# Reordering SyncE's transfers and two attention stretches in a fused retention and bilinear FFN kernel

## The chip, the cores and the metric

One core of a Trainium2 chip. The metric is the time of the whole kernel on the device in microseconds (us). The profile times one execution in detail; its span is about 1.7 us shorter than the time measured around the kernel. The granted clock of TensorE is listed for each execution.

## The reference, cut to what matters

```python
# q, k, v: (8, 8, 576, 64) float32;  w_a, w_b: (512, 1536);  w_out: (1536, 512)
scores = scale * q @ k.T
ret = (scores * Dmat) @ v              # Dmat: gamma_h ** (i - j) for i >= j, else 0
x = ret.transpose(0, 2, 1, 3).reshape(4608, 512)
out = (x @ w_a) * (x @ w_b) @ w_out
```

## The kernel before

The FFN's products run in blocks of tokens (512, 256, 256, then 512 each). The attention of a *pair* (256 tokens of all heads) is placed among them by a list `todo`: each entry has a position, counted in full FFN products of 512 columns, and is emitted at the first edge at or after it. The prediction names products by their output: for each `F`, one of the 12 groups of 128 hidden columns, `pa` and `pb` are x times the two first weights; `po` is an output tile, 12 products over `F`. An edge lies behind each `pb` and behind every fourth product of a `po`. One pair goes through these steps:

- `load_pair`: q, k, v from HBM, issued on SyncE;
- `ahead`: GpSimd casts q, then k, to bf16, and scales v (the three in this order);
- `turn`: two DMA transposes (of q, then of k), also issued on SyncE;
- `stretch(into, outof)`: TensorE's small products, for two pairs at once.

```python
    def turn(n):
        ...
        for w in (0, 1):
            nc.sync.dma_start_transpose(
                qkT[:, w].rearrange("p k c s -> p (k c) s"), qkb[:, w])

    def stretch(into, outof):
        flush()
        ...
            from_states(outof, o, begun)                  # o <- qkT, states
            ...
            convert, convert_swapped = keyed(into, ...)   # kv <- vb, qkb
            masked = matched(into)                        # sc <- qkT, qkT
            ...
            scaled = from_keys(outof, o, begun)           # o <- sT, vb
            later.append(lambda: scaled(0))               # VectorE: xT <- o, a few products later
            later.append(lambda: scaled(1))
```

So the stretch of pairs 6 and 5 needs pair 6's scaled v for `keyed` and its transposes for `matched`, and it makes the x of pair 5, which block 3 (the first of 512 tokens after the two of 256) reads at its start.

## Time and profile before

| kernel before | |
|---|---|
| time, median of 3 (lowest to highest) | 333.75 us (333.65 to 334.54) |
| span of the profiled execution | 331.8 us |
| TensorE busy | 96% |
| its waits for data in the middle of the run | 1.32 us (pair 4's transposes), 1.38 us (block 3's x) |
| granted clock, mean of the profiled execution | 1.0 |
| time in 30 later executions, beside the experiments | 332.34 to 336.36 us |

A line of the timeline has the start, the length, the engine, what it does, and in brackets how long the engine sat idle before it and what ended that. SPq is SyncE issuing transfers. The lines on which the argument stands are in the prediction.

### The profile page before, as it was taken

What the parts mean: (1) busy time and instruction counts of PE and PEld (TensorE: products, weight loads), DVE (VectorE), ACT (ScalarE), POOL (GpSimd) and SP (SyncE); (2) the same over time, 40 slices, a digit from 0 to 9 for tenths busy, and PEclk for the clock granted to TensorE, in tenths of its full rate; (3) what the DMA queues carried; (4) which work ended last, traced back from release to release, by engine and by line L of the source; (5) the groups of instructions that cost most, each with busy time, mean ns of one, the idle gap of its engine ahead of it and who ended that gap; (6) DMA issues with size and microseconds to landing.
All of it is one profiled execution on the core that took longest, in us unless ns stands there. A gap on an engine that the chain in (4) does not pass through costs nothing.

```text
span 331.8 us, 8671 instructions
## 1 busy us (share of the span) xinstructions
PE 319.8 (96%) x3612; PEld 168.1 (51%) x3648; DVE 163.7 (49%) x292; ACT 128.6 (39%) x275; POOL 114.6 (35%) x146
## 2 busy tenths in 40 slices
PE   8999999989989999999999999999999999999996
PEld 4644456848634554545454545454445444444443
DVE  5734435664674465656265625662456246414321
ACT  7734744553543344343235313532332333213321
POOL 4870078835277274634063405360430000000000
DMA  8999999999999998992599258945850420031013
GB/s 220 248 172 208 236 227 222 225 166 234 199 205 254 214 215 200 206 219 54 140 224 213 61 127 188 224 71 149 180 116 4 138 54 0 2 95 34 1 26 100
DMA packets 143175, 50.37 MB, mean 152 GB/s; under 512 B 124576, under 2 KB 138656, under 8 KB 143136
## 3 DMA queue, kind: packets, MB, share of 16 engines
q1 hardware_dynamic: 138384, 45.10, 65.0%
q0 software_dynamic: 4752, 4.72, 8.7%
q8 instruction: 28, 0.46, 0.6%
q14 instruction: 11, 0.09, 0.1%
HBM read 37.75 MB, written 9.44 MB: 142 GB/s over the span
## 4 chain that ended last, share of the span: by engine, by line
PE 86%; DMA 5%; SPq 2%; issue 2%; DVE 2%; ACT 1%; POOL 1%; DVEq 0%; POOLq 0%; ACTq 0%
PE po L716 27%; PE pb L697 27%; PE pa L682 26%; SPq L153 2%; DMA vf<-in_v_dram 2%; DMA qf<-in_q_dram 2%; PE o L589 2%; PE o L602 1%; DMA qkT<-qkb 1%; PE sc L563 1%; PE kv L506 1%; PE kv L359 1%; DVE sums L526 0%; POOL qkb L440 0%; PE pa L664 0%
## 5 line engine op out<-in xcount | busy, mean ns | idle before, releaser
L702 DVE TENSOR_TENSOR hT<-ha,pb 128x512 bf16<-128x512 bf16 (+1 forms) x120 | 75.8, 633 | 99.6 <-PE pb L697 95.2
L690 ACT CAST ha<-pa 128x512 bf16<-128x512 f32 (+1 forms) x120 | 64.8, 543 | 122.7 <-PE pa L682 121.5
L697 PE MATMUL pb<-xT,wb_sb 128*128 128x512 bf16 (+1 forms) x474 | 111.5, 357 | 0.4
L682 PE MATMUL pa<-xT,wa_sb 128*128 128x512 bf16 (+1 forms) x459 | 108.4, 357 | 2.8 <-DVE xT L612 1.4
L716 PE MATMUL po<-wo_sb,hT 128*128 128x512 bf16 (+1 forms) x430 | 95.0, 373 | 1.8 <-issue 1.6
L697 PEld LDWEIGHTS <-wb_sb 128*128 128x128 bf16 x480 | 46.8, 98 | 46.4 <-issue 0.3
L682 PEld LDWEIGHTS <-wa_sb 128*128 128x128 bf16 x474 | 45.5, 98 | 46.7 <-issue 1.9
L716 PEld LDWEIGHTS <-hT 128*128 128x128 bf16 x444 | 42.3, 98 | 46.8
L440 POOL CAST qkb<-qf 64x1024 bf16<-64x1024 f32 x15 | 15.4, 1029 | 85.8 <-DMA qf<-in_q_dram 85.0
L445 POOL TENSOR_TENSOR vb<-vf,vs 128x1024 bf16<-128x1024 f32 x15 | 28.5, 1901 | 12.4 <-DMA vf<-in_v_dram 6.3
L727 DVE COPY osb<-po 128x512 f32<-128x512 f32 (+1 forms) x18 | 12.2, 676 | 40.7 <-PE po L716 40.7
L725 ACT COPY osb<-po 128x512 f32<-128x512 f32 (+1 forms) x19 | 10.9, 574 | 44.4 <-PE po L716 41.5
L526 DVE TENSOR_TENSOR sums<-kv,sums 128x256 f32<-128x256 f32 x46 | 19.5, 423 | 2.8 <-PE kv L506 0.8
L612 DVE TENSOR_TENSOR xT<-o,qs 128x512 bf16<-128x512 f32 x30 | 19.6, 682 | 2.5 <-PE o L602 2.5
L572 DVE TENSOR_TENSOR sT<-sc,mask 128x512 bf16<-128x512 f32 x30 | 19.4, 680 | 0.0
L444 POOL CAST qkb<-kf 64x512 bf16<-64x512 f32 x30 | 17.6, 614 | 0.9
L444 POOL CAST qkb<-qf 64x512 bf16<-64x512 f32 x30 | 17.6, 614 | 0.7
L440 POOL CAST qkb<-kf 64x1024 bf16<-64x1024 f32 x15 | 15.5, 1033 | 4.2 <-DMA kf<-in_k_dram 3.2
L530 ACT CAST states<-sums 64x512 bf16<-64x512 f32 x26 | 16.0, 617 | 0.3
L299 POOL CAST qkb<-kf 128x512 bf16<-128x512 f32 x5 | 3.1, 613 | 20.0 <-DMA kf<-in_k_dram 20.0
L740 PE MATMUL w<-ones 128*128 128x256 bf16 (+1 forms) x36 | 8.3, 359 | 1.5 <-DVE ones L197 1.5
L563 PE MATMUL sc<-qkT 64*64 64x64 bf16 x480 | 7.4, 195 | 1.3 <-DMA qkT<-qkb 1.3
(81 smaller groups left out, 155.7 us busy)
## 6 DMA issues: line engine op xcount, KB each, us to landing
qf<-in_q_dram SPq DMA_DIRECT2D x32, 256.0 KB, 4.5
kf<-in_k_dram SPq DMA_DIRECT2D x32, 256.0 KB, 5.1
vf<-in_v_dram SPq DMA_DIRECT2D x32, 256.0 KB, 5.1
out_dram<-osb SPq DMA_DIRECT2D x25, 256.0 KB, 2.2
out_dram<-osb SPq DMA_DIRECT2D x22, 128.0 KB, 2.4
wo_sb<-in_moe_w_out_dram POOLq DMA_DIRECT2D x3, 512.0 KB, 18.0
qf<-in_q_dram SPq DMA_DIRECT2D x8, 128.0 KB, 3.2
kf<-in_k_dram SPq DMA_DIRECT2D x8, 128.0 KB, 3.5
```

The costliest lines, as they stand in the source:

```text
L440: nc.gpsimd.tensor_copy(qkb[0:64, w], t[0:64])
L444: nc.gpsimd.tensor_copy(to[:, :, 1 - r], fro[:, :, r])
L445: nc.gpsimd.tensor_tensor(vb.rearrange("p (k h d) -> p k h d", k=2, h=H), vf.rearrange("p (k h d) -> p k h d", k=2, h=H), vs2[:, 2 if n in ...
L526: nc.vector.tensor_tensor(sums[:, i], own, prev, op=ALU.add)
L530: nc.scalar.copy(to(half(1 - r)), fro(half(r)))
L572: nc.vector.tensor_tensor(sT[:, on].rearrange("p c k s -> p (c k) s"), sc[:, on].rearrange("p c k s -> p (c k) s"), mask3.unsqueeze(1).to_ ...
L612: nc.vector.tensor_tensor(x_of(t0, 128).rearrange("p c (a s) -> p c a s", a=2), o[:, :, :, kp].rearrange("p a c s -> p c a s"), qs[:, :, s ...
L682: nc.tensor.matmul(pa[:, 0:n], wa_sb[:, c, fs], xT[:, c], start=(c == 0), stop=(c == NC - 1))
L690: nc.scalar.copy(ha[:, 0:n], pa[:, 0:n])
L697: nc.tensor.matmul(pb[:, 0:n], wb_sb[:, c, fs], xT[:, c], start=(c == 0), stop=(c == NC - 1))
L702: nc.vector.tensor_tensor(hT[:, F, 0:n], has[F][:, 0:n], pb[:, 0:n], op=ALU.mult)
L716: nc.tensor.matmul(po[:, 0:width], hT[:, F, u * 128:(u + 1) * 128], wo_sb[:, F, cols], start=(F == 0), stop=(F == NF - 1))
```

## The change

The intent: SyncE's order by need. Pair 4's transposes are to come first, then pair 5's v, block 0's stores, pair 5's transposes, pair 6's loads; and since data then come sooner, two stretches are placed 14 products sooner. (In the built program block 0's first two stores still stand ahead of pair 4's transposes.)

```diff
@@ output tile of a block
-                if (u + part) % 2 == 0:
+                if n == 256 or (u + part) % 2 == 0:
                     nc.scalar.copy(osb[:, cols], po[:, 0:width])
@@ first loads
-    for n in range(FIRST, FIRST + 3):
+    for n in (FIRST, FIRST + 1):
         load_pair(n)
+    load_pair(FIRST + 2, (Q, K))
@@ todo
-             (246, stretch, (5, 4)), (280, stretch, (6, 5)),
+             (232, stretch, (5, 4)), (266, stretch, (6, 5)),
-    casts = {3: 104, 4: 104.1, 5: 143, 6: 200, 7: 250, 8: 330}
-    turns = {4: 104.2, 5: 151, 6: 210, 7: 338, 8: 345}
+    casts = {3: 104, 4: 104.1, 5: 141, 6: 200, 7: 250, 8: 330}
+    turns = {4: 104.2, 5: 145, 6: 210, 7: 338, 8: 345}
-    todo += [(150, load_pair, (6, (0, 1))), (152, load_pair, (6, (2,)))]
+    todo += [(104.3, load_pair, (5, (V,))), (145.1, load_pair, (6, (K,))),
+             (145.2, load_pair, (6, (Q,))), (145.3, load_pair, (6, (V,)))]
```

The rest of the diff (cut) only keeps a pair's tiles in a dictionary, so that q, k and v may be loaded in any order.

More of the change, by code (lines that the diff above doesn't have):

```diff
@@ L136, in load_pair @@
             return
-        paired.setdefault(n, [])
+        paired.setdefault(n, {})
         for i in which:
@@ L145, in load_pair @@
                     src[b, :, s0:s0 + m, :].rearrange("h s d -> s h d"))
-            paired[n].append(t)
+            paired[n][i] = t
     def load_step(n, hh, which):
@@ L433, in ahead @@
     def ahead(n):
-        qf, kf, vf = paired.pop(n)
+        qf, kf, vf = (paired[n].pop(i) for i in (Q, K, V))
         qkb = nat.tile([128, 2, 2 * DM], BF16, tag="qkb", name="qkb2")
```

## The prediction

> **What bounds the kernel now.** I read the busy table first, then the list of what TensorE waited for, then the timelines of TensorE, SyncE and GpSimd between 60 and 95 us, where the diff acts.
>
> ```profile
> PE 319.8 (96%) x3612; PEld 168.1 (51%) x3648; DVE 163.7 (49%) x292; ACT 128.6 (39%) x275; POOL 114.6 (35%) x146
> ```
>
> TensorE is the bound, and nothing in the diff changes how many products it makes. So the change can only win what TensorE waits, and the list of its waits over the whole span is short:
>
> ```profile
> PE w L740 <- DVE ones L197: 1.5, 1, 1.5
> PE pa L682 <- DVE xT L612: 1.4, 1, 1.4
> PE sc L563 <- DMA qkT<-qkb: 1.3, 1, 1.3
> ```
>
> The first is the start of the program, which the diff leaves alone. The other two are the prize. The TensorE timeline shows where they are (columns: start, length, then in brackets the idle time before and what ended it):
>
> ```profile
> 68.38 0.44 PE L506 MATMUL kv<-vb,qkb 64*64 64x64 bf16 x32
> 70.14 0.45 PE L563 MATMUL sc<-qkT 64*64 64x64 bf16 x32 [1.32 <-DMA qkT<-qkb]
> ...
> 90.34 0.45 PE L589 MATMUL o<-qkT,states 64*64 64x64 bf16 x32
> 90.96 0.45 PE L563 MATMUL sc<-qkT 64*64 64x64 bf16 x32
> 94.88 1.02 PE L682 MATMUL pa<-xT,wa_sb 128*128 128x512 bf16 x4 [1.38 <-DVE xT L612]
> ```
>
> At 70.14 the stretch of pairs 4 and 3 waits for pair 4's transposes. At 94.88 the first 512-token block waits for the x that the stretch of pairs 6 and 5, begun only at 90.34, hands to VectorE. The SyncE timeline shows the order in which transfers were issued:
>
> ```profile
> 61.07 1.87 SPq L142 DMA_DIRECT2D vf<-in_v_dram  x2
> 63.04 1.46 SPq L653 DMA_DIRECT2D out_dram<-osb  x2
> 64.60 3.28 SPq L471 DMA_TRANSPOSE qkT<-qkb  x2
> 67.97 3.88 SPq L653 DMA_DIRECT2D out_dram<-osb  x6
> 71.91 2.03 SPq L142 DMA_DIRECT2D qf<-in_q_dram  x2
> 73.98 1.75 SPq L142 DMA_DIRECT2D kf<-in_k_dram  x2
> 75.84 3.67 SPq L471 DMA_TRANSPOSE qkT<-qkb  x2
> 79.57 1.26 SPq L142 DMA_DIRECT2D vf<-in_v_dram  x2
> 80.93 1.51 SPq L653 DMA_DIRECT2D out_dram<-osb  x2
> 82.61 3.40 SPq L471 DMA_TRANSPOSE qkT<-qkb  x2
> ```
>
> These are v of pair 5, stores, pair 4's transposes, stores, q and k of pair 6, pair 5's transposes, v of pair 6, stores, pair 6's transposes. GpSimd turns pair 6 into bf16 as it lands:
>
> ```profile
> 77.38 1.03 POOL L440 CAST qkb<-qf 64x1024 bf16<-64x1024 f32 x1 [8.35 <-DMA qf<-in_q_dram]
> 79.75 1.03 POOL L440 CAST qkb<-kf 64x1024 bf16<-64x1024 f32 x1
> 84.17 1.90 POOL L445 TENSOR_TENSOR vb<-vf,vs 128x1024 bf16<-128x1024 f32 x1 [2.16 <-DMA vf<-in_v_dram]
> ```
>
> So pair 6 is cast by 82.0 and its values are ready at 86.1; its transposes, issued at 82.61 and 84.52, land at 88.6. Its stretch needs them at 90.96: the slack there is only 2.4 us, and the diff spends it from both sides.
>
> **What the Trainium skill says.** "DMA: Bandwidth & Descriptors", section "Anatomy of one DMA": the DMA engines do not wait on semaphores; the wait stands on the issuing sequencer before dispatch. So a transpose that waits for GpSimd holds everything behind it on SyncE, as the gaps before the transposes here suggest. The same page, "Queues, rings and completion order": each engine consumes a ring in order[...]. The trace agrees: from 57 to 91 us SyncE's transfers land in the order of issue, and a 256 KB load about every 1.0 to 1.2 us. "Advanced Engine Details and Errata", section "X-Bar Transpose (TRN2)": transposes are as fast as regular transfers. The trace agrees roughly: from issue to landing 3.2 to 4.9 us, median 4.1, against 3.8 to 6.1 for loads of q. "TensorE: Matmul & The Clock Gate", "What's actually happening": the clock halves after an idle window of some 3.4 us. The waits here are shorter, the granted clock is 1.00, and sixteen 512-column products take 3.45 us, 0.216 us each.
>
> **The change part by part.** The counts of instructions stay. What moves:
>
> (a) v of pair 5 goes from ahead of pair 4's transposes to behind them. The two loads took the queue from 64.08 (k of pair 5 landed) to 66.19, so 2.1 us. Pair 4's transposes should land at 70.10 - 2.1 = 68.0. The scores could start at about 68.38 + 0.35 = 68.73 (the 0.35 is the distance from kv to scores in the stretch at 90.6). So the wait of 1.32 us goes, with 0.7 us to spare: **-1.3 us**. v of pair 5 lands near 70.5 and is scaled by 72.5; it is needed at about 76.7. No cost.
>
> (b) Pair 5's transposes go ahead of q and k of pair 6: issued at about 71.9 and 73.5, landing at about 75.5 and 76.9.
>
> (c) The stretch of pairs 5 and 4 goes from 246 to 232 products. It can only be placed at an edge, every 4 full products after a pb: it moves from behind the eighth to behind the fourth F of its block. The block began at 74.25, after (a) at 72.93; four F of 0.873 us put the stretch at 76.4 and its scores at about 77.0. The transposes of (b) land at 76.9 give or take 0.6. It just fits; I count **+0.2 us**.
>
> (d) The stretch of pairs 6 and 5 goes from 280 to 266, which is from F=3 of the second output tile to F=3 of the first, 12 products or 2.6 us. Without new waits it would start at 90.34 - 1.32 - 2.59 = 86.4. VectorE then has 20 products (4.3 us) before block 3. In the trace it takes 94.88 - 91.66 = 3.2 us from the stretch's end to x, and the copy of the output tile amid it moves to ScalarE. So the wait of 1.38 us goes: **-1.4 us**.
>
> (e) Pair 6's loads come behind pair 5's transposes, k ahead of q. The work in the queue up to q's end is the same as that up to pair 5's transposes before (81.43), so q lands at about 81.2 instead of 77.27, 3.9 us later. GpSimd casts q first and cannot start with k. Its casts keep their lengths: q 81.3 to 83.6, k to 86.0 (each 1.03 + 1.17 us and small gaps), values to 87.9. The second transpose, of k, is issued at 86.1, no sooner, and lands some 3.4 us later (the lag of the second transposes at 78.27 and 104.62 is 3.2 to 3.4): 89.5. The stretch wants its values at 86.7 and its scores at 86.4 + 0.6 = 87.0. It waits first for the values, 1.3 us, then for the transposes, **+2.5 us in all**. A wait that (c) adds is absorbed here, so it isn't counted twice.
>
> (f) The output copies of the 256-token blocks all go to ScalarE: two of 0.59 us instead of 0.69 us on VectorE. ScalarE is 39% busy; off the path.
>
> Sum: -1.3 - 1.4 + 2.5 = -0.2 us. Behind 95 us TensorE waited for almost nothing, so shifts there reach the end one to one. Pair 7's loads come 1.5 us later; its stretch is at 372 products, beyond 110 us, so that is hidden. The ledger says 333.75 - 0.2 = 333.55.
>
> **The rivals.** First: the order is right and pair 6 makes it; both waits go and none comes, 333.75 - 2.7 = 331.05. For it: the author had "need" in mind, and SyncE's issue was held up by a full queue in parts of 61 to 72 us (the same kind of load takes 0.57 to 2.2 us to issue), so all may run a microsecond sooner. Against: the chain q landed, cast q, cast k, transpose is 4.7 + 3.4 us long and would have to begin at 78.9. Second: the new wait is longer than what is won. If pair 5's transposes land late at 78 and push pair 6's loads too, or pair 6's transposes wait until GpSimd has done the values (87.9) and land at 91.5, the wait is over 4 us, and the time 335.3. A wait of that length could also brush the clock window. Third: pair 4's transposes are not sooner since the stores ahead of them set the pace; then (a) wins nothing and the gain in (d) is eaten all the same: 334.9.
>
> **Range and chances.** I put half on the ledger, 0.3 on the first rival or a half of it, 0.2 on the others, and lean a little to the better side: 333.2. The range is 330.8 to 335.2. Two per cent is 6.7 us; all waits that can be won make 2.7, so faster by over 2% is excluded in practice, and slower would need a wait of 9 us in pair 6's stretch. 0.01, 0.97, 0.02.
>
> **What would show it.** In the profile after: no wait of scores for qkT near 69 us and none of pa for xT at block 3 (a, d); pair 4's transposes landing near 68.0; GpSimd's first cast of pair 6 at about 81.3 and its values done at 87.9 (e); and a new wait in the stretch at about 86.5, of kv for vb and then of scores for qkT, together 2.5 us. If that wait is under 1 us, step (e) is wrong, by q's landing or by the transposes' lag. If the two old waits are still there, (a) or (d) is. If time moves behind 95 us, I missed a dependence of pair 7.

## The result

| | before | changed |
|---|---|---|
| time, median of 4 | 333.70 us | 338.02 us (336.27 to 338.87) |
| ratio | | 1.0121, 95% interval 1.0074 to 1.0168 |
| span of the profiled execution | 331.8 us | 335.9 us |
| mean granted clock of the four executions | 1.0 where profiled | 0.988, 0.990, 0.995, 0.990 |

Ratios, here and below, are the mean time of one kernel's runs over that of the other's of the same rounds, so not quite the ratio of the medians. The changed kernel is 1.2% slower: within 2%, but outside my range. A period of half clock, 3.41 us of some 335, takes 0.005 off the mean: so the execution with 0.995, the quickest (336.27 us), had one such period, the other three (337.6 to 338.87 us) two.

The list of TensorE's waits in the changed kernel (us in total, times, longest) has lost both old entries and got two new ones, 3.5 us together:

```profile
PE kv L506 <- POOL vb L445: 2.2, 1, 2.2
PE sc L563 <- DMA qkT<-qkb: 1.3, 1, 1.3
```

TensorE's timeline after the change: pair 4's scores at 68.58 and block 3 at 98.18 no longer wait; the stretch of pairs 6 and 5 begins at 86.46 and stands still twice.

```profile
68.58 0.56 PE L563 MATMUL sc<-qkT 64*64 64x64 bf16 x32
...
86.46 0.44 PE L589 MATMUL o<-qkT,states 64*64 64x64 bf16 x32
89.14 0.64 PE L506 MATMUL kv<-vb,qkb 64*64 64x64 bf16 x32 [2.23 <-POOL vb L445]
91.05 0.64 PE L563 MATMUL sc<-qkT 64*64 64x64 bf16 x32 [1.27 <-DMA qkT<-qkb]
...
98.18 1.03 PE L682 MATMUL pa<-xT,wa_sb 128*128 128x512 bf16 x4
```

SyncE's timeline after the change has the new order. Between 82.89 and 84.81 SyncE issues nothing: it waits for GpSimd before pair 6's first transpose.

```profile
61.77 2.76 SPq L471 DMA_TRANSPOSE qkT<-qkb  x2
64.59 2.31 SPq L142 DMA_DIRECT2D vf<-in_v_dram  x2
...
70.93 3.31 SPq L471 DMA_TRANSPOSE qkT<-qkb  x2
74.30 1.25 SPq L142 DMA_DIRECT2D kf<-in_k_dram  x2
75.60 1.90 SPq L142 DMA_DIRECT2D qf<-in_q_dram  x2
77.54 3.51 SPq L142 DMA_DIRECT2D vf<-in_v_dram  x2
81.15 1.74 SPq L653 DMA_DIRECT2D out_dram<-osb  x2
84.81 4.77 SPq L471 DMA_TRANSPOSE qkT<-qkb  x2
```

GpSimd's timeline after the change: it casts pair 6 from 82.54 on, where before it began at 77.38; its last line ends at 89.09, which is what kv waited for.

```profile
82.54 1.03 POOL L440 CAST qkb<-qf 64x1024 bf16<-64x1024 f32 x1 [10.06 <-PE pa L682]
84.84 1.03 POOL L440 CAST qkb<-kf 64x1024 bf16<-64x1024 f32 x1
87.19 1.90 POOL L445 TENSOR_TENSOR vb<-vf,vs 128x1024 bf16<-128x1024 f32 x1
```

(The releaser named in the first line, a product of TensorE, computes nothing that this cast reads; q of pair 6 landed at 82.39.) The chain that ended last runs over the same cast and the second transpose (start, length): issued at 87.14, landed at 91.01.

```profile
85.94 1.18 POOL qkb L444 x2
87.14 3.87 DMA qkT<-qkb
```

And there is a line on the page of the changed kernel that the page before does not have, the granted clock in 40 slices of 8.4 us:

```profile
PEclk9999999999779999999999999999999999999999
```

The clock's records put the drop at 88.91 us, to exactly 0.50, for 6.83 us, until 95.74. Asked for the three periods around it, the window view gives TensorE's busy time and, behind the engines, the granted clock:

```profile
85.50:88.91 3.41, 1.35 (x36) 0.64 (x36) 0.74 (x2) 0.38 (x2) 3.27 (x4) 1.00 0.70 109
88.91:92.32 3.41, 1.71 (x96) 1.57 (x97) 1.77 (x5) 0.00 (x0) 0.18 (x1) 0.50 0.88 139
92.32:95.74 3.42, 3.28 (x8) 1.22 (x8) 2.41 (x4) 0.05 (x1) 1.20 (x2) 0.50 1.23 233
```

TensorE was busy for 1.35 of 3.41 us; from the end of that period on it worked at half rate, and it got its full rate back only after a period with 3.28 us of work. From pair 6's scores to block 3's first product, 91.05 to 98.18, it took 7.13 us; e1_fill and e5_six (below) do the same work at full rate in 4.97 us. So the half clock cost about 2.2 us. (The products of kv were slowed too, from 0.44 to 0.64 us, but a wait follows them, so that cost nothing.) The ledger of the span: 331.8 - 2.7 (both old waits) + 3.5 (the new ones) + 2.2 (half clock) + 0.7 (a gap of 0.89 us at 127.73, for which no cause shows, where the kernel before has 0.16) = 335.5, against 335.9 measured; for the last 0.4 us I have no place.

### The profile page after: what moved, and what is told of

Read it like the earlier page. It is cut to its first block, busy times and chain, and to the rows that moved or that the text cites. A ratio compares the mean times of both kernels' runs of the same rounds, so it can differ in the third digit from the quotient of the medians.

```text
span 335.9 us, 8671 instructions
## 1 busy us (share of the span) xinstructions
PE 322.2 (96%) x3611; PEld 169.4 (50%) x3648; DVE 162.1 (48%) x290; ACT 129.2 (38%) x277; POOL 114.6 (34%) x146
## 4 chain that ended last, share of the span: by engine, by line
PE 93%; issue 2%; DMA 1%; DVE 1%; POOL 1%; ACT 1%; ACTq 0%; DVEq 0%; POOLq 0%
PE po L716 28%; PE pb L697 27%; PE pa L682 26%; PE w L740 2%; PE o L602 2%; PE o L589 1%; PE sc L563 1%; DMA qkT<-qkb 1%; PE kv L359 1%; PE kv L506 1%; PE tp L316 1%; PE sc L331 1%; POOL qkb L444 1%; PE o L409 1%; PE pa L664 0%
## 5 line engine op out<-in xcount | busy, mean ns | idle before, releaser
L716 PE MATMUL po<-wo_sb,hT 128*128 128x512 bf16 (+1 forms) x430 | 96.6, 378 | 2.7 <-issue 2.5
L440 POOL CAST qkb<-qf 64x1024 bf16<-64x1024 f32 x15 | 15.4, 1029 | 87.0 <-DMA qf<-in_q_dram 76.9
L725 ACT COPY osb<-po 128x512 f32<-128x512 f32 (+1 forms) x21 | 12.1, 575 | 53.0 <-PE po L716 50.0
L727 DVE COPY osb<-po 128x512 f32<-128x512 f32 (+1 forms) x16 | 10.8, 674 | 40.6 <-PE po L716 40.6
L631 ACT COPY fence<-o 128x2 f32<-128x2 f32 x15 | 2.4, 160 | 16.6 <-PE o L589 16.6
```

The costliest lines, as they stand in the source:

```text
L440: nc.gpsimd.tensor_copy(qkb[0:64, w], t[0:64])
L716: nc.tensor.matmul(po[:, 0:width], hT[:, F, u * 128:(u + 1) * 128], wo_sb[:, F, cols], start=(F == 0), stop=(F == NF - 1))
```

## The experiments

Theory A: pair 6's chain (q landed, q cast, k cast, transpose landed) has become later while its stretch has become earlier; the wait of 3.5 us that follows exceeds the 2.7 us won, and the idle time in it halves the clock for a while, which costs some 3 us more. Rivals: the clock has nothing to do with it (B), the stretch of pairs 5 and 4 is to blame too (C), or the new order as such is the loss. (The 3 us were an estimate from the 6.83 us at half rate; the runs showed 2.2.) Twelve kernels ran. All outputs are right. This table sums up their profiled executions: TensorE's waits for data in the middle of the run, the periods of 3.41 us at half clock in that execution (a drop that begins after the last FFN product is not counted; such a drop takes up to 0.002 off a mean), and the time over all executions.

| run | pair 4 | pair 5 | pair 6 | block 3 | half-clock periods | span | median time (n) | ratio to before (95%) |
|---|---|---|---|---|---|---|---|---|
| before | 1.32 | 0 | 0 | 1.38 | 0 | 331.8 | 333.70 (4) | 1 |
| changed | 0 | 0 | 3.50 | 0 | 2 | 335.9 | 338.02 (4) | 1.0121 (1.0074 to 1.0168) |
| e1_fill | 0 | 0.84 | 1.07 + fill | 0 | 0 | 333.9 | 335.74 (4) | 1.0045 (0.9986 to 1.0105) |
| e2_qfirst | 0 | 0 | 2.45 | 0 | 1 | 333.2 | 334.14 (4) | 1.0020 (0.9960 to 1.0081) |
| e3_order | 0 | 0 | 0.44 | 0.22 | 0 | 329.4 | 331.25 (4) | 0.9927 (0.9882 to 0.9973) |
| e4_stretch | 1.01 | 3.66 | 0 | 0 | 1 | 337.2 | 339.32 (4) | 1.0168 (1.0113 to 1.0223) |
| e5_six | 0 | 0 | 2.79 in four parts | 0 | 0 | 332.2 | 333.65 (4) | 1.0026 (0.9938 to 1.0114) |
| e6_five | 0 | 0 | 0.70 | 0 | 0 | 330.1 | 332.58 (4) | 0.9971 (0.9913 to 1.0030) |
| e7_272 | 0 | 0 | 0.93 | 0 | 0 | 330.2 | 333.51 (4) | 0.9991 (0.9922 to 1.0060) |
| e8_vonly | 0 | 0 | 0 | 0.76 | 0 | 330.0 | 332.26 (4) | 0.9951 (0.9905 to 0.9998) |
| e9_276 | 0 | 0.20 | 0.82 | 0 | 0 | 331.0 | 332.05 (6) | 0.9944 (0.9916 to 0.9971) |
| e10_fill5 | 1.04 | 1.75 + fill | 0 | 0 | 1 | 337.0 | 338.65 (4) | 1.0141 (1.0108 to 1.0175) |
| e11_copies | 0.42 | 0 | 0 | 0.76 | 0 | 330.1 | 333.06 (6) | 0.9980 (0.9951 to 1.0008) |
| e12_both | 0 | 0 | 1.36 | 0 | 0 | 330.9 | 332.45 (6) | 0.9960 (0.9928 to 0.9992) |

### e1_fill: keep TensorE busy in the wait

The edit, shortened (`sc` is the score tile):

```diff
+            if into in FILL: fill(sc, FILL[into][0])     # FILL = {6: (9, 5)}
             convert, convert_swapped = keyed(into, outof is None)
+            if into in FILL: fill(sc, FILL[into][1])     # dummies into the score tile, which
             masked = matched(into, sc)                   # matched() then overwrites
```

> The changed kernel, with 14 dummy 512-column products (0.216 us each) in the stretch of pairs 6 and 5: nine between the old states' products and kv, where TensorE waited 2.2 us, five between kv and the scores, where it waited 1.3 us. They fit into the waits and make nothing sooner. Theory A (the wait is 3.5 us and the idle time in it lets the granted clock fall to a half for 6.8 us, which costs another 3.4 us): the waits shrink to some tenths of a us, the clock stays at 1.00, the chain of pair 6 lands as before, and the time falls from 338.0 to 333.75 - 2.7 + 3.5 = 334.5, give or take 0.6. Theory B (the half clock comes from something else, or the records of it mean nothing for the time): the time stays at 337 to 339.

Measured: 335.74 us; the granted clock was 0.999 to 1.0 in all four executions, against 0.988 to 0.995 in the four of the changed kernel. TensorE's timeline of this run, with the dummies where it stood still:

```profile
87.25 2.12 PE L557 MATMUL sc<-ones 128*128 128x512 bf16 x9
90.44 0.45 PE L506 MATMUL kv<-vb,qkb 64*64 64x64 bf16 x32 [1.07 <-POOL vb L445]
90.81 1.25 PE L557 MATMUL sc<-ones 128*128 128x512 bf16 x5
92.00 0.45 PE L572 MATMUL sc<-qkT 64*64 64x64 bf16 x32
...
96.97 1.03 PE L697 MATMUL pa<-xT,wa_sb 128*128 128x512 bf16 x4
```

In this execution pair 6 was even later (its second transpose landed at 91.68, against 91.01), and still the kernel was faster: all four executions (334.22 to 336.03 us) lie below all four of the changed kernel (336.27 to 338.87). From the start of pair 6's scores to block 3's first product it took 96.97 - 92.00 = 4.97 us, against 98.18 - 91.05 = 7.13 in the changed kernel: the same work, 2.16 us less. e5_six has the stretch at the same place and no drop either: 94.87 - 89.90 = 4.97. e2_qfirst, one period of half clock: 96.19 - 90.00 = 6.19. So theory B falls: the half clock comes from the idle time and costs about 1.2 us when it lasts one period and 2.2 us when it lasts two. (From the scores to the end of the run the two kernels differ by 244.85 - 241.9 = 2.95 us, but 0.7 us of that is the gap at 127.73, which this run doesn't have.) My 334.5 was missed by 1.2 us because the chain came later than in the run it was worked out from; the intervals of the two ratios overlap, and it is the clock records and these distances that decide.

### e2_qfirst: q before k

```diff
-(145.1, load_pair, (6, (K,))), (145.2, load_pair, (6, (Q,)))
+(145.1, load_pair, (6, (Q,))), (145.2, load_pair, (6, (K,)))
```

> The changed kernel with pair 6's loads in the order q, k, v instead of k, q, v. If the chain q landed, q cast, k cast, transpose is what makes pair 6 late: q lands near 79.0, its cast runs while k comes, k lands near 82.4 and is cast by 84.7, the second transpose is issued at 84.8 and lands at 88.7, the values are ready at 86.7. The stretch then waits 1.6 us for the scores' transposes and not for the values, too little for the clock to fall: 333.75 - 2.7 + 1.6 = 332.6. If the order of q and k does not matter (the queue as a whole is late): 337 to 338.

Measured: 334.14 us, between the two values named (332.6, and 337 to 338). GpSimd began pair 6 at 79.83 instead of 82.54, and the values were ready almost in time (0.26 us of wait). The second transpose was issued at 85.37 (84.8 expected) and landed at 89.96 (88.7 expected); it took 4.6 us. Two of the four executions had a clock of 0.999 to 1.0 (333.35 and 333.38 us), two 0.995 (334.91 and 336.48 us). So the order of q and k was a part of the changed kernel's loss (k first gains nothing, since GpSimd casts q first; the intervals of the two ratios just overlap), and a wait of 2.19 us in one piece was enough for a drop, which I had ruled out; how long the two quick executions waited, no trace shows. In the profiled one the period before the drop looks like this:

```profile
85.94:89.36 3.42, 1.62 (x68) 0.87 (x66) 1.82 (x6) 0.16 (x1) 1.38 (x1) 1.00 1.03 113
```

### e3_order and e4_stretch: one half of the change each

e3_order is the changed kernel with `(246, stretch, (5, 4)), (280, stretch, (6, 5))`; e4_stretch is the kernel before with 232 and 266. Both have the output copies on ScalarE.

> SyncE's new order alone (and the output copies on ScalarE), the two stretches back at 246 and 280. Pair 4's wait of 1.3 us goes, pair 6's stretch starts near 89.0 and waits 1.4 us for transposes that land at 91.0, and block 3 waits about 0.8 us for x: 333.75 - 1.3 + 1.4 - 0.6 = 333.2, clock 1.00. If instead the new order itself is the loss, wherever the stretches are: 337 or more.

Measured: 331.25 us, 2 us better than expected and clearly faster than before. What was left of its waits:

```profile
PE sc L563 <- DMA qkT<-qkb: 0.4, 1, 0.4
PE pa L682 <- DVE xT L612: 0.2, 1, 0.2
```

I had counted 1.4 and 0.8 us there. The transposes landed at 89.62 instead of 91.0, and VectorE sums kv while TensorE waits for the scores, so the two waits overlap instead of adding. The new order, together with the copies on ScalarE, is not the loss but a gain; the copies alone (e11_copies, ratio 0.998) are not clear of no change.

> The two stretches sooner alone (and the output copies on ScalarE), SyncE's order as before. The wait for pair 4 stays (1.3 us), pair 5's stretch wants its transposes at about 78.3 and they land at 81.4, so 3.1 us of wait; pair 6 is in time, and block 3 doesn't wait: 333.75 + 3.1 - 1.4 = 335.5 if the clock stays, up to 338.9 if the wait of 3.1 us, too, takes the clock to a half for two periods of 3.4 us.

Measured: 339.32 us, granted clock 0.985 to 0.995: the slowest of all. Pair 5's scores waited 3.66 us. In the profiled execution the period of 77.93 to 81.34 had 0.06 us of TensorE work and the next one ran at half clock. There is also a gap of 2.26 us at 96.94 for which the profile shows no wait. A fetch of 16 KB on the instruction queue, begun at 94.1 and lasting 1.3 us, lies at its start; in the kernel before the like fetches came at 88.7 and 93.2. But the changed kernel has such a fetch at 94.0, also of 1.3 us, and TensorE works through it. So the cause of this gap stays open.

### e5_six and e6_five: which stretch

The new order, with (5, 4) at 246 and (6, 5) at 266, and with 232 and 280.

> SyncE's new order, and of the two stretches only that of pairs 6 and 5 sooner (266); that of pairs 5 and 4 stays at 246. Theory A (pair 6's chain ends near 90 to 91 whatever TensorE does, so 12 products moved behind the stretch come after its end instead of before): 331.25 + 2.6 - 0.2 = 333.6 without the clock, and about 337 with one or two periods of half clock. Theory C (the stretch of pairs 5 and 4 at 232 is part of the loss): clearly under 335.

Measured: 333.65 us. Three executions between 333.02 and 333.9 with a clock of 0.998 to 1.0, just the 333.6 that the products moved behind pair 6's end account for; the fourth had 0.990, so two periods of half clock, and took 337.72. The wait is 2.8 us, hardly shorter than in the changed kernel, but here it comes in four parts (0.38, 0.57, 0.42 and 1.42 us, the first two for VectorE's and ScalarE's remains of the stretch before), and its two periods keep the clock:

```profile
84.70:88.12 3.42, 2.06 (x50) 1.07 (x51) 2.84 (x6) 2.48 (x6) 3.15 (x4) 1.00 0.96 124
88.12:91.54 3.42, 2.00 (x101) 1.36 (x101) 2.49 (x6) 0.00 (x0) 0.00 (x0) 1.00 0.69 153
```

So the drop is no sure consequence of the late chain, but depends on how the idle time falls into the clock's periods. By the values that I had put down, this run doesn't tell theory A without a drop (333.6) from theory C (clearly under 335).

> SyncE's new order, and only the stretch of pairs 5 and 4 sooner (232); that of pairs 6 and 5 stays at 280. Theory A: no more than a few tenths of wait for pair 5's transposes, taken from the wait for pair 6: 331.3, give or take 0.5, clock 1.00. Theory C: 333 or more.

Measured: 332.58 us, clock 0.998 to 1.0, between the values named. The stretch of pairs 5 and 4 at 232 waits for nothing itself. With the new order, the four combinations of the two moves took 331.25 (neither), 332.58 (5, 4), 333.65 (6, 5) and 338.02 us (both). Alone, the move of (5, 4) costs 1.3 us at the median, with overlapping intervals; on top of the other it costs 4.4. So theory C is not refuted: the loss comes from the two moves together. Of the 3.7 us between the profiled executions of e5_six and the changed kernel, 2.2 are the half clock and 0.7 the longer wait. That the earlier stretch of (5, 4) does this by leaving no other waits that would break up the idle time is argued from the four parts in e5_six, not shown.

### e7_272: half the way

The new order, (5, 4) at 246 and (6, 5) at 272.

> As e5_six, but the stretch of pairs 6 and 5 at 272, 4 products later than at 266 (which falls to the edge at 268) and 8 before 280. By theory A the scores begin when pair 6's transposes land, so each product moved behind them costs 0.216 us: 331.25 + 8 x 0.216 - 0.2 = 332.8 where the clock stays, 334.5 where it falls for one period of 3.4 us. The wait is then about 2.2 us, in the range in which the run with q first fell in two of four executions, so I expect a mixture of both values.

Measured, as expected, a mixture, though wider than the 332.8 and 334.5 named: 331.93 and 331.83 us with a clock of 1.0, 335.36 and 335.08 us with 0.995. The profiled execution is a quick one (wait 0.93 us, transposes landing at 89.09). The slow ones are 3.3 us longer; one period of half clock costs at most half of its 3.41 us, so their waits must have been longer as well, which no trace shows.

### e8_vonly and e11_copies: the smallest parts of the gain

e8_vonly undoes all but the move of pair 5's v (casts and turns of pair 5 at 143 and 151, `(150, load_pair, (6, (Q, K)))`, `(152, load_pair, (6, (V,)))`, stretches at 246 and 280) and keeps the copies on ScalarE. e11_copies is the kernel before with the one line of the copies.

> The kernel before with one transfer moved: v of pair 5 behind block 0's first stores and pair 4's transposes (and the output copies on ScalarE); pair 6's loads and both stretches as before. If that alone is what the new order wins (pair 4's wait of 1.3 us, and 0.7 us or more of block 3's wait by the copy that leaves VectorE), it takes 331.3, as e3_order did, with q of pair 6 landing near 77. If putting pair 5's transposes ahead of pair 6's loads wins something as well: 332 or more.

> The kernel before, with only the output copies of the 256-token blocks put on ScalarE. The copy of 0.69 us lies in VectorE's way between the stretch's end and x, so block 3's wait falls from 1.38 to about 0.7 us and pair 4's stays: 333.45 - 0.7 = 332.8. If ScalarE has become the one that is late there: 333.4 or more.

Measured: 332.26 and 333.06 us. In e8_vonly pair 4's wait is gone and block 3's is 0.76 us; by its median it sides with the second answer (332 or more), but its ratio, 0.9951, has an interval that overlaps that of e3_order. So that putting pair 5's transposes ahead of pair 6's loads wins anything is not shown. In e11_copies block 3's wait is 0.76 us as well, as worked out, and pair 4's is 0.42 us instead of 1.32 although nothing was done for it, so that wait swings by itself; the time (ratio 0.998) is not clear of no change.

### e9_276, e12_both: trying for a better version

e9_276 is e8_vonly with the stretch of pairs 6 and 5 at 276; e12_both is e3_order with q ahead of k.

> A version from what the runs showed: e8_vonly (pair 6's loads ahead of pair 5's transposes, as before the change) with the stretch of pairs 6 and 5 at 276 instead of 280. In e8_vonly pair 6's transposes landed at 87.3 and the scores began at 89.7, so 4 products sooner (0.86 us) still find them there, and the 0.76 us that block 3 waited for x should go: 332.3 - 0.8 = 331.5, at best 331.0 (before, less both its waits), clock 1.00. If block 3's wait stays: 332.3.

> The best so far (e3_order: the new order, stretches at 246 and 280) with pair 6's loads in the order q, k, v. GpSimd then casts q while k comes, so pair 6's transposes are issued about 1.5 us sooner, and the 0.4 us for which e3_order still waited for them should go; block 3's wait of 0.2 us for x may stay: ratio to the kernel before 0.991 to 0.993, clock 1.00 in all executions. If the transposes land as late as with k first: 0.993, as e3_order.

Measured: 332.05 us (ratio 0.9944) and 332.45 us (0.996), both faster than before and neither better than e3_order's 0.9927 (the intervals overlap); for e12_both I had expected 0.991 to 0.993. So with the later stretches the order of q and k wins nothing that shows. In both, pair 6's second transpose took longer than hoped (issued at 85.27, landed at 90.25; issued at 86.70, landed at 90.88), and a wait of 0.8 and 1.4 us came back. Each product by which a stretch is moved forward is paid back when this landing swings by a microsecond.

### e10_fill5: the clock at the other stretch

e4_stretch with the dummies of e1_fill, `FILL = {5: (0, 15)}`.

> e4_stretch (old transfers, both stretches sooner), with 15 dummy 512-column products in the wait of 3.7 us for pair 5's transposes. Theory A (idle time in a period of the clock takes it to a half, at whichever stretch it falls): the clock stays at 1.00 and the time falls by 1.4 to 3.4 us from 339.3, to 336 to 338; the wait itself stays, now filled. Theory B: 339 as e4_stretch.

Measured: 338.65 us, a miss. Here the transposes landed later (83.04 against 81.61), the dummies ended 1.75 us too soon, and the clock fell to a half for one period in three of the four executions. The fourth kept a clock of 1.0 and was no faster than 338.27. The time is nearer theory B's 339 than theory A's 336 to 338, but theory A's condition, a clock that stays at 1.00, was met by one execution alone. So this run neither confirms nor refutes that the clock cost much in e4_stretch; if anything it speaks for little.

## Why the prediction was wrong, point by point

- **(a)** Right. Pair 4's wait went away; its scores began at 68.58 (predicted 68.73).
- **(b), (c)** Right. Pair 5's transposes landed at 76.32 (76.9) and its scores began at 77.08 (77.0) without a wait. In e1_fill the same spot waited 0.84 us: it just fits, no more.
- **(d)** Right. The stretch began at 86.46 (86.4), and block 3 did not wait.
- **(e)** The mechanism was right and the size was not. q landed at 82.39 (81.2), because I let the queue be as quick as before; so the second transpose was issued at 87.14 (86.1). Its lag was 3.87 us; I had taken 3.4 us from two of the quicker transposes, although the same view gave a median of 4.1. It landed at 91.01 (89.5), the values were done at 89.09 (87.9), and the wait was **3.5 us, not 2.5**.
- **The step that failed** is the sentence on the clock, "The waits here are shorter, the granted clock is 1.00". It was true of the two waits that were there, each alone, and I carried it over to a wait that I predicted myself. The term is missing from the sum altogether; the second rival only has it "brush the clock window" above 4 us. It measured 2.2 us (7.13 us against e1_fill's 4.97 for the same work). With (e) at 3.5 us alone the ledger's 333.55 becomes 334.55, still inside my range; the clock's 2.2 us make it about 336.8, against 336.27 to 338.87 measured.
- **(f)** Right: no wait for the copies on ScalarE shows. And as (d) counted on, with VectorE relieved of the copy, block 3's wait is 0.76 us instead of 1.38 (e11_copies).
- **"Behind 95 us ... shifts there reach the end one to one."** Nearly: a gap of 0.7 us without a visible cause came on top.
- **The weights.** I leaned to the better side of my own ledger for the author's intent. The trace spoke for a chain without slack, and that the stretch's 2.4 us of slack were "spent from both sides" stood in my text; the lean had no number behind it.

## What to carry to other kernels

When a transfer moves later and its reader moves earlier, follow the whole chain (landing, both casts, transpose, landing) with median lags, not the quickest; here the first half of the change, alone (e3_order, the copies included), is 0.7% faster than the kernel before, and the second half turns that into 1.2% slower. In these traces a wait of TensorE cost more than its length once TensorE was busy for half of a clock period of 3.41 us or less (with the exceptions listed below): count the idle time per period, and if it can't be removed, products that need nothing can fill it, as in e1_fill.

## What the Trainium skill lacked or had wrong

- "TensorE: Matmul & The Clock Gate", section "What's actually happening" (half rate after an idle window of about 3.4 us) and section "Why this matters for your kernels" (no idle gaps above about 3 us): a gap of 2.19 us (e2_qfirst), or one of 2.23 us with 1.27 us after it (changed kernel), was enough here; the period was not idle. From the instruction and clock records, periods with TensorE busy for 0.02 to 0.50 of the time were followed by half clock (five periods in four kernels: 0.02, 0.40, 0.47, 0.49, 0.50), periods with 0.59 and more kept the full clock. Two periods do not fit, since they kept it: e4_stretch from 95.00 to 98.42, busy 0.43, all of it with full-size products, and e2_qfirst at its end, from 328.29 to 331.70, busy 0.46, with products of `po`. Where the threshold lies, and whether small products count less, stays open.
- The same page gives the period as free-running: that fits, since all drops in the middle of a run last 3.41 or 6.83 us. That the same kernel falls in some executions and not in others (e2_qfirst, e7_272: two of four each) would follow from it, but their waits may have differed too. The page tells of such a variation for the clock's rise at the start of a kernel; for drops in the middle of a run no page has it. Here executions of one kernel differed by up to 4.7 us (e5_six: 333.02 to 337.72), of which two periods of half clock account for some 2.2.
- "Advanced Engine Details and Errata", section "X-Bar Transpose (TRN2)" states the speed of transposes but not how far it swings: in these traces the transposes of pairs 4 to 6, all of one size, took 3.1 to 6.0 us from issue to landing.
